# Attention and two token mixtures on one core: preparing the 16 weight blocks of the first mixture on GpSimd in place of ScalarE

## The chip, the cores and the metric

One core of one Trainium2 chip runs the whole program. The metric is the device time of one execution in microseconds (us). The engines are called PE (TensorE, matrix products), PEld (its weight loads), DVE (VectorE), ACT (ScalarE), POOL (GpSimd) and SP (SyncE, which issues most transfers).

## The reference

```python
# 4 batches, 8 heads, 576 tokens, 64 per head; width 512
scores = q @ k.T / 8 + min(-(cum_i - cum_j), 0)      # causal, cum = cumsum(max(s, 0))
x = softmax(scores) @ v                              # heads joined: (4, 576, 512)
h = max(x @ w_in, 0)                                 # first mixture: w_in 512x1024, float64
x = (h * sigmoid(conv3(h))) @ w_out                  # w_out 1024x512, float64
u = x + (x.T @ U @ V).T                              # second mixture: rank 32 along tokens
out = u + max(u @ w_ch1, 0) @ w_ch2                  # 512x2048 and 2048x512, float64
```

The weights of both mixtures arrive as 64-bit floats, so each is read as two 32-bit words and turned into a float32 on the chip. For the products a float32 is split in a high part (rounded to the type fp32r) and a low part (what is left), and three products of the parts are summed.

## The kernel before, in words

The kernel first describes its whole work as a list of operations, each with an engine, an estimated cost and the buffers it reads and writes. A planner then runs a list schedule over it: an engine that becomes free takes, among the operations whose inputs are there by the planner's own clock, the one that stands earliest in the list. The order that comes out is written into each engine's queue and stays fixed: on the chip an engine executes its queue in that order and waits at the head if an input is late. So a changed cost or engine of a few operations can move all others.

The 32 heads of the attention are worked in turn by `att_head(h)`: scores on PE (`products`, line 675, and `last_rows`, line 691), minimum over a row on DVE (`top`, line 636), exponentials on ACT (`exps`, line 653), sums and reciprocals on DVE (lines 726, 727, 768 and 774), multiplication of a row by its reciprocal on POOL (`normalise`, line 664, the tiles P0 to P3 of a head and one tile p for each pair of heads), transposes on PE (line 798), copies of these on ACT (`hi_act`, line 352, tile th), and the products with v (line 824). The x of a pair of heads is split in xh on ACT and xl on POOL (`lo_pool`, line 364). From head 8 on the q and k of a pair are split too: high part on POOL (line 355), low part on DVE (line 361). Eight heads fill one batch; then `m1_in` (line 868) and `m1_out` (line 910) do the first mixture of that batch among the heads of the next.

The weights w_in and w_out of the first mixture come as 16 blocks of 128 x 512 (f = 0 to 7, the columns 0 and 512 of each). `load_split` brings one after the heads that the list W1_AT names (heads 0 to 8 for the first ones, the last four after heads 10 and 11). For each block it does this, in a chain:

1. a transfer of 512 KB into `raw`, of which there are two;
2. `decode64`: the high word of each element, every second 32-bit word of `raw`, is multiplied in place by 2 to the -111 on ACT (line 501); then three integer operations on DVE (line 504 once, line 514 twice) put the float32 together in `wf`, of which there are two as well;
3. `hi_act` (line 352) casts `wf` to the high part on ACT;
4. `lo_pool` (line 364) subtracts the high part from `wf` on POOL.

The high and low parts are w1h and w1l for w_in, and both are called w1o for w_out. `decode64` also serves the weights of the rank-32 step, the convolution and the second mixture, and `load_split` the w_ch2 blocks of the second mixture.

Of the kernel before, what the change touches and what calls it, by code (L numbers as in the profile page):

```python
# [8 lines left out]
F32 = mybir.dt.float32  # L9
# [5 lines left out]
ALU = mybir.AluOpType  # L15
# [293 lines left out]
def tile_attention_moe_mixer(  # L309
# [14 lines left out]
    nc = tc.nc  # L324
# [3 lines left out]
    def dve(n, fn, r, w, fast=False):  # L328
        return plan.op("DVE", (155 if st.get("late") else 70) + n * (0.52 if fast else 1.042), fn, r, w)

    def act(n, fn, r, w, extra=0):
        return plan.op("ACT", (157 if st.get("late") else 53) + n * 0.834 + extra, fn, r, w)

    def pool(n, fn, r, w, two=False, extra=125):
        return plan.op("POOL", ((280 if st.get("late") else 148) + n * 2.1) if two else (37 + n * 0.834 + extra), fn, r, w)

    def dma(nbytes, fn, r, w):
        return plan.op("SP", 640, fn, r, w, late=nbytes / 360)
# [12 lines left out]
    def hi_act(out, src, r, w, n):  # L351
        act(n, lambda: nc.scalar.copy(out(), src()), r, w)  # L352
# [10 lines left out]
    def lo_pool(out, src, hi, r, w, n):  # L363
        pool(n, lambda: nc.gpsimd.tensor_tensor(out(), src(), f32(hi()), ALU.subtract), r, w, two=True)  # L364
# [15 lines left out]
    def ring(pool_, cls, count, shape, dtype, name, at={}):  # L380
        n = at[pool_, cls] = at.get((pool_, cls), -1) + 1
        return pool_.buf(f"{cls}{n % count}", shape, dtype, name)
# [42 lines left out]
    w1h, w1l = {}, {}  # L425
# [59 lines left out]
        o.preds.add(scan)  # L485


    def decode64(out, okeys, raw, n):

        def half(i, dt):
            return raw().bitcast(dt).rearrange("p (n two) -> p n two", two=2)[:, :n, i]

        def oi():
            return out().bitcast(I32)

        act(n, lambda: nc.scalar.mul(half(1, F32), half(1, F32), 2.0**-111), [raw], [(raw, 1)], 40)  # L501
        dve(
            n,
            lambda: nc.vector.tensor_scalar(  # L504
                oi(), half(1, I32), 3, 0x7FFFFFF8, ALU.logical_shift_left, ALU.bitwise_and
            ),
            [(raw, 1)],
            okeys,
            True,
        )  # L510
        for i, sc, op in ((0, 29, ALU.logical_shift_right), (1, -0x80000000, ALU.bitwise_and)):
            dve(
                n,
                lambda i=i, sc=sc, op=op: nc.vector.scalar_tensor_tensor(  # L514
                    oi(), half(i, I32), sc, oi(), op, ALU.bitwise_or
                ),
                [(raw, 1), *okeys],
                okeys,
            )

    def load_split(src, h, l, c, n, name):

        raw = ring(dec, "raw", RINGS["w64"], [128, 512], I64, f"raw_{name}")
        load = dma(n * 1024, lambda: nc.sync.dma_start(out=raw[:, :n], in_=src[:, c : c + n]), [], [raw])
        load.preds.add(st["first"])
        wf = ring(dec, "wf", RINGS["wf"], [128, 512], F32, f"wf_{name}")
        decode64(lambda: wf[:, :n], [wf], raw, n)
        hi_act(lambda: h[:, :n], lambda: wf[:, :n], [wf], [h], n)
        lo_pool(lambda: l[:, :n], lambda: wf[:, :n], lambda: h[:, :n], [wf, h], [l], n)

    def load_cw():
        raw = ring(dec, "raw", RINGS["w64"], [128, 512], I64, "raw_cw")
        dma(24576, lambda: nc.sync.dma_start(out=raw[:, :24], in_=cwU[:, :24]), [], [raw])
        decode64(cw, [cw], raw, 24)
        pool(24, lambda: nc.gpsimd.tensor_scalar(cw(), cw(), 2.0**-8, 1.0, ALU.mult, ALU.mult), [cw], [cw])

    def load_mixu():
        raw = ring(dec, "raw", RINGS["w64"], [128, 512], I64, "raw_mix")
        wf = ring(dec, "wf", RINGS["wf"], [128, 512], F32, "wf_mix")
        dma(163840, lambda: nc.sync.dma_start(out=raw[:, :160], in_=cwU[:, 24:184]), [], [raw])  # L540
        decode64(lambda: wf[:, :160], [wf], raw, 160)
        act(160, lambda: nc.scalar.mul(wf[:, :160], wf[:, :160], 2.0**-8), [wf], [wf])

        def u():
            return wf[:, :160].rearrange("p (a b) -> p a b", b=32)

        hi_dve(lambda: uhl[:, :, 0:32], u, [wf], [(uhl, 0)], 160)
        lo_dve(lambda: uhl[:, :, 32:64], u, lambda: uhl[:, :, 0:32], [wf, (uhl, 0)], [(uhl, 1)], 160)

    def load_mixv(c):  # L550

        raw = ring(dec, "raw", RINGS["w64"], [128, 512], I64, f"raw_v{c}")
        wf = ring(dec, "wf", RINGS["wf"], [128, 512], F32, f"wf_v{c}")
        sl = slice(c, c + HS)
        dma(294912, lambda: nc.sync.dma_start(out=raw[:, :HS], in_=mixV[:, sl]), [], [raw])
        decode64(lambda: wf[:, :HS], [wf], raw, HS)
        act(HS, lambda: nc.scalar.mul(wf[:, :HS], wf[:, :HS], 2.0**-8), [wf], [wf])
        hi_act(lambda: vs[:, sl], lambda: wf[:, :HS], [wf], [(vs, c)], HS)
        low = slice(64, 128)
        lo_dve(  # L560
            lambda: vs[low, sl], lambda: wf[low, :HS], lambda: vs[low, sl], [wf, (vs, c)], [(vs, c)], HS
        )
# [747 lines left out]
    def att_head(h):  # L1310

        if h + 1 < NH:
            if h % 2 == 1:
                prep_v(h + 1)
            if h + 1 in FS:
                prep4(h + 1)
            else:
                if h % 2 == 1:
                    prep(h + 1)
                place(h + 1)  # L1320
        if h == 1:
            decay_parts()
            for t in qkBs:
                clear(t)
        for i in range(2):
            if h < NH:
                scores(h, i)
        if h > 0:
            transp(h - 1, 0)
        if h < NH:  # L1330
            scores(h, 2)
        if h > 0:
            transp(h - 1, 1)
            if h % 2 == 0:
                av(h - 2, 0)
        if h < NH:
            scores(h, 3)
        if h > 0:
            transp(h - 1, 2)
            transp(h - 1, 3)  # L1340
        if h < NH and h % 2 == 0:
            scores4(h)
        if h > 0 and h % 2 == 0:
            av(h - 2, 1)
# [11 lines left out]
    def m1_parts(b):  # L1356

        out = []
        prev = []
        if b:  # L1360
            prev = [(WP, lambda dt=dt: m1_out(b - 1, 1, dt)) for dt in range(KT)]
            last = [(WM, t) for t in mix_parts(b - 1)]
        for f in range(NF1):
            out.append((WI, lambda f=f: m1_in(b, 0, f)))
            if b:
                out += prev[2 * f : 2 * f + 2] if f < 2 else last[2 * f - 4 : 2 * f - 2]
        for f in range(NF1):
            out.append((WI, lambda f=f: m1_in(b, 1, f)))
            if f >= 4:
                out.append((WO, lambda f=f: m1_out(b, 0, f - 4)))  # L1370
        return out

    for h in range(NH + 1):
        b, hh = divmod(h - 1, H)
        todo = []
        if b >= 1:
            parts = m1_parts(b - 1)
            whole = sum(w for w, t in parts)
            at, todo = 0, []
            for w, t in parts:  # L1380
                if hh <= at * H / whole < hh + 1:
                    todo.append(t)
                at += w
        att_head(h)
        for n, (f, c) in enumerate(w1_jobs):
            if h == W1_AT[n]:
                load_split(w1[f], w1h[f, c], w1l[f, c], c, 512, f"w1_{f}_{c}")
        if h == CW_AT:
            load_cw()
        if h == MIX_AT:  # L1390
            load_mixu()
            for c in (0, HS):
                load_mixv(c)
        for t in todo:
            t()
# [82 lines left out]
    for g in range(2):  # L1478
        blk = (w2a, u1p)[g].buf(f"u{g}", [128, 2 * 7 * S], F32R, f"w2_{g}")
        for i in range(7):  # L1480
            f = 7 * g + i
# [3 lines left out]
    def load_w2b(f):  # L1485
        load_split(w2[f], w2h[f], w2l[f], 512, 512, f"w2b_{f}")
# [84 lines left out]
```

## Time and profile before

| | |
|---|---|
| median of 3 runs | 833.66 us (832.91 to 836.38) |
| the profiled execution | 831.95 us, of which 830.2 us is the span from the first to the last instruction |
| granted TensorE clock, mean | 0.996 of full speed |
| PE busy | 791.6 us |
| DVE, ACT, POOL busy | 538.2, 454.3, 360.0 us |

The profile is one execution, recorded instruction by instruction. A busy time counts only executing instructions; the idle time before an instruction is put down to what released it. The ends of matrix products are modelled, so that a PE that counts as busy can still be waiting a little.

### The profile page before, as it was taken

To read this page: it belongs to the slowest core of one execution; us is meant where nothing else is said; L and a number is where in the kernel's file an instruction comes from. 1 tells how busy PE (TensorE), PEld (TensorE's weight loads), DVE (VectorE), ACT (ScalarE), POOL (GpSimd) and SP (SyncE) were. 2 spreads that over 40 slices of the span, in tenths; PEclk is the share of its full clock that TensorE was granted. 3 is DMA by queue.
4 is the path that set the end of the run, shared out by engine and by line. 5 is a ranking of instruction groups with operands and counts; after the bars stand their busy time and mean duration, and the time that the engine had idled before them with its cause. 6 is when DMAs were issued, how large, how long until landed. Compare 5 with 4: busy or idle time off the path is not lost. (4 is left out here: it accounts for less than half of the span.)

```text
span 830.2 us, 15394 instructions
## 1 busy us (share of the span) xinstructions
PE 791.6 (95%) x5300; PEld 709.2 (85%) x5300; DVE 538.2 (65%) x1182; ACT 454.3 (55%) x1144; POOL 360.0 (43%) x441
## 2 busy tenths in 40 slices
PE   4898899999999999999989999999999999999998
PEld 2566788999899999999988898999998888888888
DVE  6887797636855378556998989777688632323232
ACT  4897898858878488767656334324344322222212
POOL 4786684634537234383284776455564200000000
PEclk9999999999999999999999999999999999999999
DMA  7657755734466247030235335446378563636443
GB/s 212 184 170 192 167 154 149 167 97 107 142 144 156 60 111 208 5 109 1 85 109 181 126 133 191 162 150 191 123 220 301 154 193 100 189 103 184 114 127 98
DMA packets 66310, 119.70 MB, mean 144 GB/s; under 512 B 9396, under 2 KB 34868, under 8 KB 66232
## 3 DMA queue, kind: packets, MB, share of 16 engines
q1 hardware_dynamic: 66160, 118.70, 49.7%
q8 instruction: 42, 0.69, 0.4%
q14 instruction: 36, 0.29, 0.1%
q10 hardware_dynamic: 72, 0.01, 0.0%
HBM read 68.81 MB, written 28.90 MB: 118 GB/s over the span
## 5 line engine op out<-in xcount | busy, mean ns | idle before, releaser
L1252 PE MATMUL my<-mh,w 128*128 128x512 f32 (+1 forms) x560 | 158.8, 368 | 0.0
L1153 PE MATMUL ma_S<-u,W 128*128 128x288 f32 x768 | 120.5, 298 | 5.0 <-DVE s L1169 5.0
L1233 DVE SCALAR_TENSOR_TENSOR ml<-ml,mh 128x512 fp32r<-128x512 f32 (+1 forms) x80 | 53.1, 672 | 105.2 <-ACT mh L1230 105.0
L1230 ACT ACTIVATE mh<-ml 128x512 fp32r<-128x512 f32 (+1 forms) x80 | 46.9, 589 | 128.3 <-DMA ml<-ch_d 76.9
L1252 PEld LDWEIGHTS my<-mh,w 128*128 128x128 f32 x560 | 101.7, 189 | 17.5
L910 PE MATMUL y<-gh,w1o 128*128 128x288 f32 x512 | 114.2, 301 | 1.1 <-POOL w1o L364 1.0
L1153 PEld LDWEIGHTS ma_S<-u,W 128*128 128x128 f32 x768 | 108.3, 189 | 7.2 <-DVE s L1169 7.1
L664 POOL TENSOR_SCALAR P<-P,sm 128x128 f32<-128x128 f32 (+3 forms) x128 | 77.1, 618 | 80.3 <-DVE sm L727 63.2
L1252 PE MATMUL my<-ml,w 128*128 128x512 f32 (+1 forms) x280 | 103.0, 368 | 0.0
L1153 PE MATMUL ma_A<-u,W 128*128 128x288 f32 x576 | 92.5, 295 | 0.9 <-ACT p L1165 0.9
L636 DVE CUSTOM_DVE_ANT_0 sc<-sc,mask 128x128 f32<-128x128 f32 (+2 forms) x144 | 68.6, 498 | 34.5 <-PE sc L675 32.5
L910 PEld LDWEIGHTS y<-gh,w1o 128*128 128x128 f32 x512 | 85.0, 188 | 2.2 <-POOL w1o L364 1.3
L364 POOL TENSOR_TENSOR gl<-c,gh 128x288 fp32r<-128x288 f32 x64 | 53.5, 841 | 74.7 <-ACT gh L895 64.4
L868 PE MATMUL h<-xh,w1h 128*128 128x290 f32 x256 | 80.9, 316 | 3.0 <-ACT P L653 0.9
L1153 PEld LDWEIGHTS ma_A<-u,W 128*128 128x128 f32 x576 | 82.0, 188 | 1.6 <-ACT p L1165 1.1
L880 DVE SCALAR_TENSOR_TENSOR c<-h,cw,c 128x288 f32<-128x288 f32 x128 | 64.4, 512 | 26.9 <-ACT c L876 25.8
L868 PE MATMUL h<-xl,w1h 128*128 128x290 f32 x256 | 76.9, 300 | 0.2 <-POOL xl L364 0.2
L868 PE MATMUL h<-xh,w1l 128*128 128x290 f32 x256 | 76.5, 299 | 0.0
L910 PE MATMUL y<-gl,w1o 128*128 128x288 f32 x256 | 74.8, 292 | 0.0
L653 ACT ACTIVATE P<-sc,sm 128x128 f32<-128x128 f32 (+3 forms) x128 | 67.7, 532 | 10.6 <-DVE sm L636 9.2
L352 ACT COPY th<-pt 128x384 f32<-128x384 f32 (+2 forms) x128 | 63.1, 493 | 8.7 <-PE pt L798 7.7
L798 PE MATMUL pt<-ident,P 128*128 128x128 f32 x320 | 59.9, 275 | 1.4 <-ACT th L352 0.8
(139 smaller groups left out, 1734.4 us busy)
## 6 DMA issues: line engine op xcount, KB each, us to landing
ml<-ch_d SPq DMA_DIRECT2D x64, 256.0 KB, 2.8
ch_d<-p SPq DMA_DIRECT2D x64, 144.0 KB, 1.8
raw_w<-w_in SPq DMA_DIRECT2D x16, 512.0 KB, 4.5
raw_w2a<-w_in SPq DMA_DIRECT2D x16, 512.0 KB, 4.8
raw_w2b<-w_in SPq DMA_DIRECT2D x16, 512.0 KB, 4.3
t<-qk_in SPq DMA_DIRECT2D x24, 288.0 KB, 3.1
qkB<-t SPq DMA_DIRECT2D x24, 288.0 KB, 3.8
qkA<-t SPq DMA_DIRECT2D x24, 288.0 KB, 3.9
```

What stands on the lines that cost most here:

```text
L352: act(n, lambda: nc.scalar.copy(out(), src()), r, w)
L364: pool(n, lambda: nc.gpsimd.tensor_tensor(out(), src(), f32(hi()), ALU.subtract), r, w, two=True)
L636: lambda: nc.vector.tensor_tensor_reduce(out=ps[:rows, :w], in0=ps[:rows, :w], in1=mask[:rows, m0 : m0 + w], scale=-0.125, scalar=3.0e38 i ...
L653: lambda: nc.scalar.activation(out(), ps[:rows, :w], ACTF.Exp, bias=low(), scale=-1.0, accum_out=total()),
L664: lambda: nc.gpsimd.tensor_scalar(t[:, :w], t[:, :w], r(), 1.0, ALU.mult, ALU.mult),
L798: nc.tensor.transpose(pt[:, o + rows - 128 : o + rows], d["P"][i][:, 128 * j : 128 * j + 128], turn)
L868: nc.tensor.matmul(ps[:, :W], lhsT=ww, rhs=xx, start=kt + n == 0, stop=kt == KT - 1 and n == 2)
L880: lambda k=k: nc.vector.scalar_tensor_tensor(c(), hh[:, k : k + HS], cw[:, 3 * f + k : 3 * f + k + 1], c(), ALU.mult, ALU.add),
L910: nc.tensor.matmul(ps[:, :HS], lhsT=ww, rhs=xx(), start=f + n == 0, stop=f == NF1 - 1 and n == 2)
L1153: nc.tensor.matmul(ps[:, :HS], lhsT=ww, rhs=uu, start=k == 0, stop=k == 5)
L1233: lambda: nc.vector.scalar_tensor_tensor(ml[:, :n], raw(), 0.0, f32(mh[:, :n]), ALU.max, ALU.subtract),
L1252: nc.tensor.matmul(ys[c][dt][:, :n], lhsT=ww, rhs=xx[:, :n], start=f + k == 0, stop=f == NF2 - 1 and k == 2)
```

## The change

For the 16 blocks of the first mixture alone, the multiplication by 2 to the -111 and the cast to the high part are done by POOL, as `tensor_scalar` instructions with two constants. The three DVE operations, the subtraction on POOL, the transfers and every other use of the two functions stay. The planner is given the costs of `pool(n, ...)` for both, 589 ns for 512 columns, in place of 520 and 480 ns on ACT. Its order of the whole program is made anew from these.

```diff
-    def decode64(out, okeys, raw, n):
+    def decode64(out, okeys, raw, n, spare=False):
...
-        act(n, lambda: nc.scalar.mul(half(1, F32), half(1, F32), 2.0**-111), [raw], [(raw, 1)], 40)
+        if spare:
+            pool(
+                n,
+                lambda: nc.gpsimd.tensor_scalar(half(1, F32), half(1, F32), 2.0**-111, 1.0, ALU.mult, ALU.mult),
+                [raw],
+                [(raw, 1)],
+            )
+        else:
+            act(n, lambda: nc.scalar.mul(half(1, F32), half(1, F32), 2.0**-111), [raw], [(raw, 1)], 40)
...
-    def load_split(src, h, l, c, n, name):
+    def load_split(src, h, l, c, n, name, spare=False):
...
-        decode64(lambda: wf[:, :n], [wf], raw, n)
-        hi_act(lambda: h[:, :n], lambda: wf[:, :n], [wf], [h], n)
+        decode64(lambda: wf[:, :n], [wf], raw, n, spare)
+        (hi_pool if spare else hi_act)(lambda: h[:, :n], lambda: wf[:, :n], [wf], [h], n)
...
-                load_split(w1[f], w1h[f, c], w1l[f, c], c, 512, f"w1_{f}_{c}")
+                load_split(w1[f], w1h[f, c], w1l[f, c], c, 512, f"w1_{f}_{c}", True)
```

## Rows read from the trace of the kernel before

**Rows 1.** The page's busy time, share of the span and instructions of each engine.
```profile
PE 791.6 (95%) x5300; PEld 709.2 (85%) x5300; DVE 538.2 (65%) x1182; ACT 454.3 (55%) x1144; POOL 360.0 (43%) x441
```

**Rows 2.** Busy time by stretch: from:to, length, each engine (instructions), clock, DMA share.
```profile
40.00:60.00 20.00, 18.83 (x125) 12.10 (x125) 16.66 (x48) 18.24 (x51) 16.07 (x21) 1.00 0.57 167
...
83.00:87.00 4.00, 3.68 (x17) 3.67 (x18) 1.39 (x4) 3.11 (x10) 3.12 (x5) 0.57 1.04 207
...
20.00:125.00 105.00, 92.65 (x628) 71.08 (x629) 86.62 (x231) 90.04 (x250) 75.41 (x90) 0.98 0.66 172
...
100.00:125.00 25.00, 22.69 (x167) 20.05 (x164) 22.82 (x56) 23.25 (x63) 20.76 (x22) 1.00 0.56 148
125.00:420.00 295.00, 293.94 (x2230) 271.52 (x2229) 187.77 (x507) 216.84 (x594) 137.32 (x203) 1.00 0.43 113
```

**Rows 3.** Waits of PE, 20 to 125 us: total, times, longest.
```profile
PE pt L798 <- ACT P L653: 2.8, 4, 1.8
...
PE y L910 <- POOL w1o L364: 1.0, 1, 1.0
...
PE h L868 <- ACT x L837: 0.3, 1, 0.3
```

**Rows 4.** ACT by line and shape, 8 to 125 us: busy, mean ns.
```profile
L501 ACT ACTIVATE raw_w<-raw_w 128x512 f32<-128x512 f32 x16 | 11.9, 754 | 0.3 <-DMA raw_w<-w_in 0.2
...
L352 ACT CAST w1o<-wf_w 128x512 fp32r<-128x512 f32 x8 | 5.0, 620 | 1.9 <-DVE wf_w L514 1.9
L352 ACT CAST w1h<-wf_w 128x512 fp32r<-128x512 f32 x8 | 5.0, 619 | 1.2 <-DVE wf_w L514 1.2
```

**Rows 5.** Instructions of single lines or tiles: duration in ns, shortest/median/longest.
```profile
L664 POOL TENSOR_SCALAR p<-p,sm x6: 739/788/1703, 18.2 to 103.3; 128x576 f32<-128x576 f32 x6
...
L355 POOL TENSOR_SCALAR t<-t x8: 670/676/1167, 19.1 to 124.0; 128x576 fp32r<-128x576 f32 x8
...
L364 POOL TENSOR_TENSOR w1l<-wf_w,w1h x8: 1264/1276/1462, 20.2 to 57.0; 128x512 fp32r<-128x512 f32 x8
...
L504 DVE TENSOR_SCALAR wf_w<-raw_w x16: 398/440/1433, 14.9 to 117.7; 128x512 int32<-128x512 int32 x16
```

**Rows 6.** POOL in order of time: start us, us, instructions, idle before.
```profile
27.82 3.07 POOL L664 TENSOR_SCALAR P<-P,sm 128x128 f32<-128x128 f32 x4 [0.44 <-DVE sm L727]
...
35.62 1.20 POOL L364 TENSOR_TENSOR xl<-x,xh 128x576 fp32r<-128x576 f32 x1 [2.12 <-ACT xh L352]
...
40.08 2.05 POOL L664 TENSOR_SCALAR P<-P,sm 128x128 f32<-128x128 f32 x4 [1.86 <-DVE sm L727]
...
77.76 1.28 POOL L364 TENSOR_TENSOR w1o<-wf_w,w1o 128x512 fp32r<-128x512 f32 x1
```

**Rows 7.** DVE in order of time, two places.
```profile
35.68 1.43 DVE L504 TENSOR_SCALAR wf_w<-raw_w 128x512 int32<-128x512 int32 x1
...
77.83 1.84 DVE L361 TENSOR_TENSOR t<-t,t 128x576 fp32r<-128x576 f32 x1
```

**Rows 8.** PE in order of time: the seven places used, with the idle time before.
```profile
24.59 0.52 PE L798 MATMUL pt<-ident,P 128*128 128x128 f32 x3 [0.78 <-ACT th L352]
...
31.37 2.27 PE L824 MATMUL av<-th,vr 128*64 128x320 f32 x20 [0.59 <-ACT th L352]
...
38.70 0.40 PE L868 MATMUL h<-xh,w1h 128*128 128x290 f32 x1 [0.95 <-ACT P L653]
...
53.90 1.12 PE L675 MATMUL sc<-qkF 128*128 128x512 f32 x2 [0.97 <-ACT th L352]
...
81.27 0.30 PE L798 MATMUL pt<-ident,p 128*128 128x128 f32 x1 [1.83 <-ACT P L653]
...
99.64 2.27 PE L824 MATMUL av<-th,vr 128*64 128x320 f32 x20 [1.10 <-ACT th L352]
...
107.58 0.40 PE L868 MATMUL h<-xh,w1h 128*128 128x290 f32 x1 [0.92 <-ACT th L352]
```

**Rows 9.** ACT in order of time: the casts ahead of three of these places.
```profile
23.16 0.62 ACT L352 CAST w1h<-wf_w 128x512 fp32r<-128x512 f32 x1 [0.67 <-DVE wf_w L514]
...
30.37 0.62 ACT L352 CAST w1h<-wf_w 128x512 fp32r<-128x512 f32 x1 [0.53 <-DVE wf_w L514]
...
105.87 0.61 ACT L352 CAST w1o<-wf_w 128x512 fp32r<-128x512 f32 x1
```

## The prediction

> **What bounds the kernel now.** I read the page's busy times first: PE is busy for 95% of the span, no other engine above 65% [rows 1]. So the end can only move by what PE idles, or by the clock that it gets. Next I cut the span into stretches. After 125 us PE is busy for 293.94 of 295 us [rows 2]; nothing of the change happens there, and little is to be had. All 16 blocks are prepared before about 123 us, and in 20 to 125 us PE is busy for 92.65 of 105 us: 12.35 us of idle time. What the change can win on PE lies inside these 12.35 us, plus a stretch of 4 us at 0.57 of the clock (83 to 87 us, behind a PE that had idled just before), which costs 4 x 0.43 = 1.7 us. As later work on PE is back to back, a microsecond won or lost here arrives at the end.
>
> In the same 105 us ACT is busy for 90.04 (86%), DVE for 86.62 (82%) and POOL for 75.41 (72%). ACT is the most loaded of the three, which is the ground for the change. Then I read PE's waits: the eight kinds that name ACT sum to 10.1 us, from 2.8 us down to 0.3 us each, and POOL's w1o has 1.0 us [rows 3]. These names are the last link only. So I followed single idle places back through ACT, DVE and POOL in order of time; they fall in two sorts, used below.
>
> **What the change removes.** From ACT: 16 multiplications of mean 754 ns (11.9 us) and 16 casts of mean 620 ns (10.0 us) [rows 4]. About 20 us of it lies in the stretch of 105 us, so ACT falls from 86% to 67%. That by itself moves nothing; what counts is where PE waited because ACT stood at such an instruction. ACT waited 0.67 us for DVE before the cast at 23.16 us, 0.53 us before the one at 30.37 us, and did another at 105.87 us; the next copies or exponentials queued behind them, and the PE idle times at 24.59, 31.37 and 107.58 us follow [rows 8, 9]. I give the change all three: 0.78 + 0.59 + 0.92 = **2.3 us won**.
>
> **What it adds.** To POOL: 32 instructions on 128 x 512 elements. The trace has no such cast or strided multiplication there, so I bound it. The one-input instruction on 576 columns takes at least 670 ns with constants and 739 ns with a pointer [rows 5]. Four instructions with a pointer, 1280 columns together, take 2.05 us when nothing disturbs them [rows 6]; with 739 ns for 576 columns that is 0.88 ns a column and 0.23 us for each instruction. Then 64 columns fewer than 670 ns are 0.62 us, which I take for the cast. The multiplication touches every second word; nothing on POOL in this stretch does. Below, it costs 0.62 us like the cast; above, 1.26 us, like the subtraction that reads twice as many words [rows 5]. ACT's strided multiplication is dearer than its cast by 0.13 us in the mean [rows 4], and a stride adds no words to be processed, so I take 0.66 us. A block is 1.28 us, and the 15 blocks' worth in the stretch some 18.5 us. POOL rises from 75.4 to 93.9 us of 105 (89%) and takes ACT's place as the most loaded engine but PE.
>
> The Trainium skill, GPSIMD Engine Reference (Engine selection), says that one-input elementwise work on GpSimd runs at roughly line rate, and in its cycle accounting gives 769 ns for a tight loop over 512 elements; with that figure 32 instructions would be an estimated 24.6 us in place of 20.5. The shortest rows here are below it.
>
> Three costs on PE follow.
>
> First, **the shared lock**. DVE's instruction of line 504 takes 398 ns undisturbed, but 1.43 us at 35.68 us, where POOL's xl ran from 35.62 to 36.82 us; line 361 took 1.84 us at 77.83 us, beginning just behind POOL's w1o at 77.76 us [rows 5 to 7]. The reverse shows too: the same four normalising instructions took 2.05 us at 40.08 us and 3.07 us at 27.82 us, where DVE put weights together [rows 6]. Such places precede the PE idle times at 38.70, 53.90, 81.27 and 99.64 us, 4.85 us together [rows 8], through a late minimum on DVE and a late exponential or copy on ACT. They arise from 75.4 us of POOL work; 18.5 us more, in proportion, cost **1.2 us**. A lower bound is nothing (if the new work falls where DVE reads PSUM); an upper one is four times as much, if the new work, which sits right beside DVE's operations on the same block, meets them far more often.
>
> The Trainium skill, SBUF — State Buffer (Who interferes with whom), states the rule: GpSimd and a DVE instruction with two SBUF inputs or in a two-port mode take a shared port pair exclusively, and the later one blocks fully. The trace agrees with it (398 ns against 1.43 us), and it speaks against moving work to GpSimd while DVE decodes.
>
> Second, **POOL's queue at the end of the weights**. In 100 to 125 us POOL is busy for 20.76 of 25 us, which leaves 4.24; four blocks are prepared there and add 4 x 1.28 = 5.1 us. The surplus, **0.9 us**, makes the last w1o later, for which PE already waits 1.0 us [rows 2, 3]. With the locks it would be 1.9 us; at nothing, if PE has heads to work on meanwhile.
>
> Third, **normalisation behind bulk work**. The 11 sets of four normalising instructions and 5 of the p tiles in the stretch will now at times find a new instruction running: its share of time is 18.5/105 = 0.18, what is left of it on average 0.32 us, so 16 x 0.18 x 0.32 = **0.9 us**. The transposes on PE stand behind them. Nothing, where the transposes come later than that anyway.
>
> The three integer operations, the subtraction and the transfers cost what they did. A later decode makes the next transfer into `raw` later by as much, but the next block is not due for a head; if that cover went, SP's later transfers of q and k would wait too. One hop fewer between engines (cast and subtraction both on POOL) I cost at nothing: no one waits for a w1h part before 38.70 us.
>
> **Sum.** -2.3 + 1.2 + 0.9 + 0.9 = +0.7 us. The profiled execution, 831.95 us with a span of 830.2, becomes 832.65. The median of the runs is 1.71 us above the profiled one, so I predict **834.4 us**. A change of this kernel that is under 0.5% (4.2 us) can hardly be told from none, given runs from 832.91 to 836.38 us.
>
> **Rivals.**
>
> *ACT's relief wins (faster).* Exponentials and copies free PSUM banks for PE, and all of them move ahead when ACT falls to 67%. If two thirds of the 10.1 us that name ACT go, and the half-clock stretch with its 1.7 us, less 0.9 us for w1o, the gain is 6.7 + 1.7 - 0.9 = 7.5 us: 826 us. For it speaks that ACT is named most. Against it, that four of the seven places begin with DVE and POOL meeting. It decides if POOL keeps its queue: normalisation must begin as soon after the reciprocal as now (0.44 us and 1.86 us idle before it [rows 6]).
>
> *POOL becomes the bound (slower).* In 40 to 60 us POOL has 16.07 us of work [rows 2] and the four blocks there bring 5.1: 21.2 in 20 us. With the same in 100 to 125 us, the queue is over full in two stretches: 1.2 + 1.9 us; the locks at their upper bound cost 4.8 us, and normalisation behind two new instructions in place of half of one, 16 x 0.18 x 1.28 = 3.7 us. Less 2.3 us, that is +9.3 us: 843 us. It decides once POOL passes some 95% in 20 to 125 us, because then its delay no longer dies out between pairs of heads.
>
> *The strided multiplication costs as much as a subtraction (slower).* 16 x 0.6 us = 9.6 us more, POOL at 93.9 + 14 x 0.6 = 102 of 105 us before any lock. With no slack left PE bears up to all of it: 844 us. Against it, a stride adds no words.
>
> *The order shifts but the waits only change their names.* That is within my forecast: an ACT below its bound does nothing for a PE that is busy for 88% of the stretch and fed by DVE.
>
> **How the numbers follow.** Chances: my forecast (within 0.5%) 0.48, its own range 830 to 838 us; relief 0.23; POOL as the bound 0.22; dear stride 0.07. So faster 0.23, same 0.48, slower 0.29. The range goes from the relief at 826, of which I leave out the far half, to POOL as the bound at 843: 827 to 843 us, with some 0.1 left out on each side.
>
> **What would show it.** In the profile after: no raw_w and w1 instruction on ACT, ACT near 70 us in 20 to 125 us; 32 new one-input instructions on POOL of 0.62 to 0.70 us when alone; POOL above 90% there; lines 504, 514 and 361 on DVE longer in the mean than now; idle times of PE behind casts gone, and new ones that name POOL. PE's idle time to 125 us should be 13 us in place of 12.35. Wrong would be a strided instruction far from 0.66 us; a second stretch at about half the clock, or none; or a POOL that PE waits for more than three times.

## The result and the profile after

The changed kernel takes 844.25 us in the median of four runs (840.59 to 845.87), beside 835.02 us in four runs of the kernel before (832.91 to 837.54). The ratio on record is 1.0124 with the interval [1.0093, 1.0155]; the quotient of the two medians alone is 1.011, and all ratios below are those on record. The change is slower by about 1.2%, some 10 us, and lies 1.25 us above my range. The profiled execution took 840.59 us with a span of 838.8 us, 8.6 us more than before.

The page's busy times after, to be read beside [rows 1]:

```profile
PE 795.7 (95%) x5300; PEld 709.5 (85%) x5300; DVE 541.5 (65%) x1182; ACT 439.7 (52%) x1112; POOL 382.7 (46%) x473
```

ACT lost 14.6 us and POOL got 22.7 us. In the median the single instructions cost what I had worked out (0.66 us for the multiplication, 0.62 us for the cast); in the mean, with what disturbs them, it is 0.71 and 0.64 us. From line 501 on, the lines of the changed kernel are numbered 8 higher: the first operation of DVE's decode, line 504 before, is line 512, and line 504 is now POOL's multiplication (each run below has a numbering of its own). These rows of single instructions give the duration in ns, shortest/median/longest, and the first and last start:

```profile
L504 POOL TENSOR_SCALAR raw_w<-raw_w x16: 637/664/1093, 14.1 to 122.7; 128x512 f32<-128x512 f32 x16
...
L355 POOL TENSOR_SCALAR w1h<-wf_w x8: 610/616/620, 19.0 to 63.2; 128x512 fp32r<-128x512 f32 x8
...
L918 PE MATMUL y<-gh,w1o x512: 288/295/403, 125.7 to 439.3; 128*128 128x288 f32 x171
```

And in the kernel before:

```profile
L910 PE MATMUL y<-gh,w1o x512: 288/296/401, 116.3 to 429.4; 128*128 128x288 f32 x171
```

The y rows date the loss: the first y product begins at 125.7 us, and in the kernel before it began at 116.3 us; in both, 605 PE instructions stand ahead of it. That is 9.4 us, already more than the 8.6 us of the whole span. So everything is lost before some 126 us, where the weights are prepared. The busy times by stretch, with the columns of [rows 2]:

```profile
20.00:24.00 4.00, 3.58 (x15) 2.92 (x14) 3.05 (x9) 1.43 (x4) 3.18 (x6) 0.50 0.53 165
...
40.00:44.00 4.00, 4.00 (x15) 2.39 (x14) 2.91 (x9) 2.22 (x9) 3.59 (x6) 0.62 0.94 256
...
20.00:125.00 105.00, 89.35 (x576) 65.52 (x574) 81.75 (x212) 68.53 (x200) 88.42 (x109) 0.96 0.60 162
125.00:420.00 295.00, 292.12 (x2209) 268.18 (x2209) 188.39 (x513) 216.75 (x595) 140.37 (x208) 1.00 0.43 112
```

In 20 to 125 us PE's idle time grew from 12.35 to 15.65 us, and its mean clock fell from 0.98 to 0.96. Two stretches stand at the lower level of the clock or near it (the first two rows), where the kernel before has one (83 to 87 us [rows 2]). ACT fell to 65% of the stretch. POOL rose to 84%, less than I had forecast, because the same work now takes longer than the stretch. No engine but PE is above 85%, and still PE is fed less well than before. Up to the first y product PE idles 4.4 us more than before and is busy for 5.0 us more with the same 605 instructions. Of these 5.0 us the lower clock is 3.4 (5.1 us lost against 1.7), and the rest lies within time that counts as busy, whose ends are modelled. The clock's part is that of two single executions: over the runs the mean granted clock is 0.993 after and 0.992 in 23 runs of the kernel before, so, as far as is on record, the clock doesn't account for the 1.2%.

PE's waits in 20 to 125 us after (total, times, longest), beside [rows 3]:

```profile
PE sc L699 <- DMA qkF<-cc: 2.5, 1, 2.5
PE sc L683 <- ACT P L661: 2.4, 1, 2.4
PE pt L806 <- ACT P L661: 2.2, 3, 1.3
PE sc L683 <- DMA qkA<-t: 1.9, 2, 1.0
...
PE pt L806 <- POOL p L672: 0.7, 1, 0.7
```

Two kinds stand out. The waits for transfers are new (4.8 us with one of 0.4 us; none in this stretch before), and by name they are more than the 3.3 us of idle time that PE gained; those that name ACT were 10.1 us and are 9.4. And PE hardly names POOL. The engine that does is DVE:

```profile
DVE wf_w L512 <- POOL raw_w L504: 6.4, 5, 1.8
```

This is DVE's wait for the multiplication, at the head of its queue. Its size is not new: before, DVE stood 9.2 us ahead of the same operation, 6.0 of them until POOL's subtraction had read `wf` (the row of line 504 before, shown with e5). It has another cause now and stands elsewhere. The place at 38.08 us shows what it does; here are POOL, DVE, ACT and PE after in order of time (start us, us, then the instructions):

```profile
29.29 2.96 POOL L672 TENSOR_SCALAR P<-P,sm 128x128 f32<-128x128 f32 x4 [1.10 <-DVE sm L735]
...
32.23 0.99 POOL L504 TENSOR_SCALAR raw_w<-raw_w 128x512 f32<-128x512 f32 x1
...
33.25 0.84 DVE L512 TENSOR_SCALAR wf_w<-raw_w 128x512 int32<-128x512 int32 x1 [1.27 <-POOL raw_w L504]
...
34.59 1.76 POOL L364 TENSOR_TENSOR w1l<-wf_w,w1h 128x512 fp32r<-128x512 f32 x1
...
35.22 1.74 DVE L361 TENSOR_TENSOR t<-t,t 128x576 fp32r<-128x576 f32 x1
...
36.89 0.42 DVE L644 CUSTOM_DVE_ANT_0 sc<-sc,mask 128x256 f32<-128x256 f32 x1
...
37.46 0.47 ACT L661 ACTIVATE P<-sc,sm 128x256 f32<-128x256 f32 x1 [2.78 <-DVE sm L644]
...
38.08 0.49 PE L683 MATMUL sc<-qkF 128*128 128x128 f32 x2 [2.45 <-ACT P L661]
```

The multiplication stood on POOL behind four normalising instructions; DVE stood 1.27 us for it, then lost about a microsecond more where line 361 met the subtraction (1.74 us; the shortest of its kind in this kernel takes 0.74 us). A minimum over scores, which needs neither the weights nor the parts of q and k that line 361 makes, was queued behind both; ACT's exponential waited 2.78 us for it, and PE 2.45 us. PE's clock in the 4 us behind that pause was 0.62.

The transfers come by SP's queue. SP after in order of time, and the PE instruction that waits:

```profile
51.49 0.38 SPq L598 DMA_DIRECT2D vr<-vP_in  x1
56.65 0.33 SPq L532 DMA_DIRECT2D raw_w<-w_in  x1
57.07 0.51 SPq L584 DMA_DIRECT2D qkF<-qk_in  x1
57.63 0.59 SPq L586 DMA_DIRECT2D qkF<-cc  x1
58.27 1.30 SPq L591 DMA_DIRECT2D qkF<-cc  x1
...
64.40 0.67 PE L699 MATMUL sc<-qkF 128*64 128x288 f32 x2 [2.55 <-DMA qkF<-cc]
```

From 51.9 to 56.65 us SP stands at a weight transfer that waits for its buffer, that is for the decode of an earlier block (4.7 us, the longest of its kind; 15.6 us in all, 11.4 before). The q and k of the next pair are queued behind it, and PE waits for them. In the kernel before, the same q and k (the eighth of these transfers in both) went out at 50.30 to 52.55 us, ahead of the ninth weight transfer:

```profile
50.30 0.51 SPq L576 DMA_DIRECT2D qkF<-qk_in  x1
...
52.66 2.45 SPq L524 DMA_DIRECT2D raw_w<-w_in  x2
```

### The profile page after: what moved, and what is told of

Read it like the earlier page. It is cut to its first block, busy times and chain, and to the rows that moved or that the text cites. A ratio compares the mean times of both kernels' runs of the same rounds, so it can differ in the third digit from the quotient of the medians.

```text
span 838.8 us, 15386 instructions
## 1 busy us (share of the span) xinstructions
PE 795.7 (95%) x5300; PEld 709.5 (85%) x5300; DVE 541.5 (65%) x1182; ACT 439.7 (52%) x1112; POOL 382.7 (46%) x473
## 5 line engine op out<-in xcount | busy, mean ns | idle before, releaser
L661 ACT ACTIVATE P<-sc,sm 128x128 f32<-128x128 f32 (+3 forms) x128 | 67.8, 532 | 19.2 <-DVE sm L644 16.8
```

The lines of the kernel that those rows point to most:

```text
L661: lambda: nc.scalar.activation(out(), ps[:rows, :w], ACTF.Exp, bias=low(), scale=-1.0, accum_out=total()),
```

## The experiments

The expectations speak of four theories. **A**: POOL's own load costs the time, because other work waits in its queue (A1) or because it meets DVE's instructions (A2). **B**: the new order costs it, above all weight transfers ahead of q and k on SP. **C**: the multiplication is the first link of a block's chain, and DVE's decode waits for it at the head of its queue. **D**: the planner took POOL for faster than it is. A last rival is that it is ACT's relief that is worth nothing. All experiments were timed in five rounds against the kernel before; "POOL" and "PE" are busy us in 20 to 125 us of each run's profile, the same column as above. e1, e5, e9, e10, e11, e13 and e14 have PE, DVE and SP in the order of the kernel before (in e14 with the added copies), e2 in that of the changed kernel. The other eight have an order of their own, and so differ by it as well. The mean granted clock of the runs is 0.990 to 0.995 (0.992 to 0.994 in the kernel before), but 0.987 in e1 and e14 and 0.988 in e8; there a lower clock is part of the loss.

| run | ratio to before | interval | PE | POOL |
|---|---|---|---|---|
| after | 1.0124 | 1.0093 to 1.0155 | 89.35 | 88.42 |
| e1 work moved, old order | 1.0170 | 1.0145 to 1.0196 | 89.16 | 86.19 |
| e2 work on ACT, new order | 1.0149 | 1.0126 to 1.0172 | 87.01 | 67.23 |
| e3 multiplication alone | 1.0094 | 1.0070 to 1.0119 | 89.26 | 79.66 |
| e4 cast alone | 1.0043 | 1.0024 to 1.0062 | 92.56 | 85.75 |
| e5 two idle casts on POOL | 1.0126 | 1.0104 to 1.0147 | 87.06 | 86.80 |
| e6 decode planned later | 1.0058 | 1.0037 to 1.0080 | 92.36 | 97.23 |
| e7 transfers planned later | 1.0145 | 1.0121 to 1.0168 | 88.27 | 83.86 |
| e8 POOL's measured costs | 1.0153 | 1.0127 to 1.0178 | 91.67 | 80.00 |
| e9 one idle cast on POOL | 1.0085 | 1.0062 to 1.0109 | 91.28 | 81.56 |
| e10 memsets on POOL | 1.0164 | 1.0137 to 1.0191 | 87.38 | 87.26 |
| e11 no multiplication, old order | 0.9989 | 0.9970 to 1.0008 | 95.93 | 76.38 |
| e12 subtractions on DVE | 0.9986 | 0.9960 to 1.0011 | 94.97 | 60.06 |
| e13 tiny memsets on POOL | 1.0125 | 1.0092 to 1.0158 | 87.22 | 82.12 |
| e14 longer decode on DVE | 1.0133 | 1.0100 to 1.0167 | 87.93 | 67.51 |
| e15 no multiplication, new order | 1.0066 | 1.0042 to 1.0091 | 89.86 | 73.31 |
| e16 no multiplication, subtractions on DVE | 0.9938 | 0.9916 to 0.9961 | 97.41 | 61.76 |

### Engine and order taken apart (e1, e2)

e1 issues the 32 instructions to POOL, but tells the planner ACT's costs, so that PE, DVE and SP keep the order of the kernel before, instruction by instruction. e2 is the opposite: the planner is told POOL, and ACT executes; those three queues have the order of the changed kernel.

```diff
e1, against the changed kernel
-            pool(
+            act(
                 n,
                 lambda: nc.gpsimd.tensor_scalar(half(1, F32), half(1, F32), 2.0**-111, 1.0, ALU.mult, ALU.mult),
...
+                40,
...
+            act(n, lambda: nc.gpsimd.tensor_scalar(h[:, :n], wf[:, :n], 1.0, 1.0, ALU.mult, ALU.mult), [wf], [h])
e2
+            pool(n, lambda: nc.scalar.mul(half(1, F32), half(1, F32), 2.0**-111), [raw], [(raw, 1)])
...
+            pool(n, lambda: nc.scalar.copy(h[:, :n], wf[:, :n]), [wf], [h])
```

> The 32 instructions run on POOL as in the change, but the planner is told that they are ACT's, with ACT's costs: PE, DVE and SP keep exactly the order of the kernel before, and only the engine differs. Theory A (POOL itself: its queue and its meetings with DVE hold up PE): as slow as the change, 841 to 847 us, PE idle 15 us or more in 20 to 125 us. Theory B (the new order: transfers of weights stand ahead of those of q and k on SP and wait): near the kernel before, 832 to 837 us, and no wait of PE for a q or k transfer.

> The reverse: the order of the change on PE, DVE and SP, but ACT does the 32 instructions. Theory A: near the kernel before, 832 to 837 us, since POOL has its old work. Theory B: as slow as the change, 840 to 846 us, with PE waiting 4 to 5 us for q and k transfers as there.

Each is as slow as the whole change: 845.32 us (+1.7%) and 844.26 us (+1.5%). In e1, where SP issues what it did before in the same order, DVE stands still for the multiplication twice as long as after:

```profile
DVE wf_w L513 <- POOL raw_w L504: 13.5, 9, 2.7
```

So the loss, by A or by C, doesn't need the new order. In e2 POOL has its old instructions (67.23 us of them in the stretch) and ACT 78.96 us, and yet the new order costs the same; PE's waits name the transfers again:

```profile
PE sc L681 <- ACT th L352: 2.9, 3, 2.0
PE pt L804 <- ACT P L659: 2.6, 5, 1.1
PE pt L804 <- ACT th L352: 2.6, 4, 1.0
PE sc L681 <- DMA qkF<-cc: 2.2, 1, 2.2
```

Neither suits the other's conditions: an order made for POOL's timing was run with ACT's. So e2 shows what an order that doesn't fit costs, not what the order costs in the changed kernel. The two losses don't add (3.2% against 1.24%).

### The halves of the change (e3, e4)

e3 moves only the multiplication, e4 only the cast; each is planned anew.

```diff
e3, against the changed kernel
-        (hi_pool if spare else hi_act)(lambda: h[:, :n], lambda: wf[:, :n], [wf], [h], n)
+        hi_act(lambda: h[:, :n], lambda: wf[:, :n], [wf], [h], n)
e4
-        decode64(lambda: wf[:, :n], [wf], raw, n, spare)
+        decode64(lambda: wf[:, :n], [wf], raw, n)
```

> Only the 16 multiplications on POOL, the casts stay on ACT; planned anew. Theory A: POOL has half of the new work, so about half of the loss, 837 to 841 us. Theory B: the multiplication decides when raw is free, so most of the loss, 839 to 845 us, and DVE's first operation still waits for POOL.

> Only the 16 casts on POOL, the multiplications stay on ACT; planned anew. Theory A: the other half, 837 to 841 us. Theory B: the cast stands behind raw's last reader, so raw is free as early as before: 832 to 837 us.

The multiplication costs 0.94% and the cast 0.43%, for almost the same time on POOL. The multiplication stands at the head of a block's chain, with DVE's queue behind it; behind the cast comes POOL's own subtraction. This would speak for C beside A; but each has an order of its own, and the 0.5% between them may be that.

### POOL's load alone (e5, e9)

ACT keeps its work and the order stays that of before. Ahead of each subtraction POOL does two (e5) or one (e9) further casts into the buffer of the low part, which the subtraction then overwrites.

```diff
e5, against the kernel before (e9: range(1))
...
+            def low():
+                for _ in range(2):
+                    nc.gpsimd.tensor_scalar(l[:, :n], wf[:, :n], 1.0, 1.0, ALU.mult, ALU.mult)
+                nc.gpsimd.tensor_tensor(l[:, :n], wf[:, :n], f32(h[:, :n]), ALU.subtract)
...
```

> The kernel before in its own order, ACT doing its 32 instructions; POOL makes two extra casts of 512 columns into the low part ahead of each subtraction, which overwrites them. So POOL carries the load of the change, but the multiplication, DVE's decode and the cast do not wait for it. Theory A (POOL's load and its meetings with DVE): 841 us or more. Theory C (the multiplication is the first link of the chain: DVE's decode, in its fixed order, waits for POOL, and minima stand behind it): 832 to 838 us, and no wait of DVE for a multiplication.

> The kernel before in its own order, with one extra cast on POOL ahead of each of the 16 subtractions in place of two: half the load. Theory A, if POOL's load costs in proportion: half of 1.26%, 836 to 839 us. If POOL has slack up to some load: 831 to 834 us, and the loss comes with the second cast alone.

Work that nobody asked for, on an engine that was 72% busy, costs 1.26%, as much as the change; half of it costs 0.85%. One place of e5 in order of time shows how:

```profile
83.91 2.22 POOL L533 TENSOR_SCALAR w1o<-wf_w 128x512 fp32r<-128x512 f32 x2 [2.04 <-DVE wf_w L514]
...
85.57 0.15 DVE L783 RECIPROCAL sm<-sm 128x1 f32<-128x1 f32 x1
...
86.21 1.31 POOL L534 TENSOR_TENSOR w1o<-wf_w,w1o 128x512 fp32r<-128x512 f32 x1
...
87.51 1.17 POOL L673 TENSOR_SCALAR p<-p,sm 128x576 f32<-128x576 f32 x1
...
88.74 0.33 PE L807 MATMUL pt<-ident,p 128*128 128x128 f32 x1 [2.42 <-POOL p L673]
```

The reciprocal for p is there at 85.72 us. POOL is at two extra casts and the subtraction until 87.5 us, so the normalisation is 1.8 us late, and PE stands 2.42 us for it. This is A1, but only a part of the 2.42 us is new: in the kernel before the same PE instruction waits 1.83 us, for an exponential (81.27 us [rows 8]). A2 is there as well in e5: DVE's operations on the blocks get longer. In these groups from 8 to 140 us, of before, of e9 and of e5, the numbers behind the bar are busy us and the mean in ns:

```profile
L514 DVE SCALAR_TENSOR_TENSOR wf_w<-raw_w,wf_w 128x512 int32<-128x512 int32 x32 | 26.9, 842 | 0.5
L504 DVE TENSOR_SCALAR wf_w<-raw_w 128x512 int32<-128x512 int32 x16 | 10.1, 630 | 9.2 <-POOL w1l L364 4.0 <-POOL w1o L364 2.0 <-ACT raw_w L501 1.9
```

```profile
L514 DVE SCALAR_TENSOR_TENSOR wf_w<-raw_w,wf_w 128x512 int32<-128x512 int32 x32 | 28.7, 899 | 0.5
L504 DVE TENSOR_SCALAR wf_w<-raw_w 128x512 int32<-128x512 int32 x16 | 10.6, 664 | 10.0 <-issue 4.2 <-ACT raw_w L501 3.6 <-POOL w1l L533 2.1
```

```profile
L514 DVE SCALAR_TENSOR_TENSOR wf_w<-raw_w,wf_w 128x512 int32<-128x512 int32 x32 | 33.5, 1048 | 0.5
L504 DVE TENSOR_SCALAR wf_w<-raw_w 128x512 int32<-128x512 int32 x16 | 8.4, 528 | 9.9 <-POOL w1l L533 4.4 <-POOL w1o L533 2.3 <-ACT raw_w L501 2.0
```

The sum of the two is 37.0 us before, 39.3 in e9 and 41.9 in e5. In e9 line 361, which meets POOL too, got shorter (from 8.8 to 7.7 us), and the 128x4 sums stayed (314 ns each after 319), so these groups together took about 1 us more there, against 7.1 us of time (0.85%). That would speak for the queue. But PE idles only 13.72 us of the stretch in e9, 1.4 us more than before (17.94 us in e5), at a clock of 0.96 against 0.98, so its profile shows little of the queue's cost. One profile of each is what this rests on.

### Queue or meetings (e10, e13, e14)

e10 and e13 were meant to load POOL without DVE meeting it: memsets, which read nothing, in place of e5's casts (three of 512, 512 and 256 columns, or forty of two columns, overwritten again). e14 is the reverse: POOL keeps its old work, and DVE does a 320-column copy of the first integer operation once more ahead of each block.

```diff
e10, in the function of e5 (e13: forty memsets of 2 columns)
+                for m in (n, n, n // 2):
+                    nc.gpsimd.memset(f32(l[:, :m]), 0.0)
e14, against the kernel before
+            if wone:
+                nc.vector.tensor_scalar(
+                    oi()[:, :320], half(1, I32)[:, :320], 3, 0x7FFFFFF8, ALU.logical_shift_left, ALU.bitwise_and
+                )
```

> As with two extra casts, but POOL writes constants instead (512, 512 and 256 columns, some 1.3 us for each block), so it reads nothing while it is busy. Theory A1 (the queue: normalisation and subtractions stand behind the new work): 841 to 845 us, as with the casts. Theory A2 (meetings with DVE's reads): 831 to 835 us, and DVE's second and third operations on a block back at the durations of the kernel before.

> As with two extra casts ahead of each subtraction, in the order of the kernel before, but POOL makes 40 memsets of two columns instead, some 1.2 us for a block by the 0.03 us from start to start that such memsets take at the head of the kernel, so that no single one can hold DVE for long. Theory A1 (the queue): 840 to 845 us with DVE's three operations on a block at 37 us in sum, as in the kernel before. Theory A2 (meetings with DVE): 831 to 835 us.

> The kernel before in its own order, with DVE's first operation on each of the 16 blocks preceded by one on 320 columns that it overwrites: some 0.3 us for a block, 4.9 us in all, which is what the two extra casts made DVE's operations on the blocks longer. POOL's load is the old one. Theory A2 (DVE's lengthening is what PE pays for): 839 to 843 us. Theory A1: 832 to 836 us.

The memsets cost 1.64% and 1.25%. But DVE's meetings didn't stay as they were; the first operation got longer, in e10:

```profile
L504 DVE TENSOR_SCALAR wf_w<-raw_w 128x512 int32<-128x512 int32 x16 | 13.0, 811 | 10.0 <-POOL w1l L533 4.4 <-POOL w1o L533 2.4 <-ACT raw_w L501 2.0
```

With line 514 (29.4 us) the sum is 42.4 us, and 42.7 us in e13, more than in e5. Most of it isn't the memsets' doing: in e10 four of the 16 met a subtraction of these blocks and took 1.02 to 1.45 us, while of the five that met memsets alone four took 0.42 to 0.49 us, and one 0.85 us. So neither tells A1 from A2. e14 adds more to DVE than planned (7.7 us for the 16 copies, with their gaps and meetings some 9.5 us in the four groups), leaves POOL at 67.51 us, and costs 1.33%. So a delay on DVE without new work on POOL, twice as long as e5's (9.5 us against 4.9), is enough for the whole loss, in part by the lower clock of its runs; and by e9 a load on POOL with about 1 us on DVE is enough for two thirds of it. In the changed kernel itself DVE's two groups grew by only 2.4 us (28.4 + 11.0 against 37.0), so meetings are probably not its larger part; the shares stay open. A load on POOL that DVE never meets was not found.

### The plan's part (e6, e7, e8)

All three are the changed kernel with another plan. In e6 the planner believes that the multiplication's result comes 1.5 us later, so it puts other work on DVE ahead of the decode. In e7 a block's transfer is planned no earlier than the subtraction two blocks before it, so that SP has less to wait for. In e8 the planner is given POOL's costs as measured.

```diff
e6, against the changed kernel
-            )
+            ).late = 1500
e7
...
+        if spare and len(subs) > 1:
+            load.preds.add(subs[-2])
...
e8
...
+            plan.ops[-1].cost += 190
...
+                extra=254,
...
+            extra=388 if st.get("slow") else 208,
```

> The change, with the planner told that the multiplication's result arrives 1.5 us later on every other engine, so that DVE's decode is put later in its queue. Theory C: DVE's 6.4 us of waiting for the multiplication go to under 2 us and the time to 834 to 840 us. Theory A: no better than the change, 841 to 847 us, since POOL does as much.

> The change, with the transfer of a block put on SP no earlier than the planner's end of the subtraction of the block two before. Theory B (weight transfers wait on SP ahead of those of q and k): SP's 15.6 us of waiting for the decode shrink by half, PE waits for no q or k transfer, and the time is 836 to 841 us. Theories A and C: 841 to 847 us, as POOL and the decode are where they were.

> The change, with the planner given POOL's costs as the changed kernel's trace has them while weights are prepared: 718 and 644 ns for multiplication and cast, 180 ns more for each normalising instruction, 190 ns more for a subtraction. Theory D (the order is bad because the planner's POOL is too fast): 833 to 839 us. Theory A: 841 to 847 us.

e6 gives back half of the loss (0.58% remains): DVE's wait for the multiplication falls from 6.4 to 2.0 us, POOL reaches 97.23 of 105 us, and PE 92.36 us, almost what it had before. That agrees with C for about half; but e6 has a new order throughout, and what that is worth by itself isn't shown. e7 cuts SP's wait for the decode from 15.6 to 5.6 us, but POOL then waits 6.5 us for the blocks, and the time stays at +1.45%. PE still waits 5.2 us for q and k there, so e7 didn't remove what B speaks of:

```profile
PE sc L689 <- DMA qkB<-t: 3.1, 1, 3.1
...
PE sc L705 <- DMA qkF<-cc: 2.1, 1, 2.1
```

That B isn't needed for a loss is shown by e1, where PE waits for no transfer in the stretch; how much it is in the changed kernel stays open. e8 doesn't help either (+1.53%): POOL waits 6.5 us for blocks there too, PE 7.7 us for q and k, and PE's clock in the stretch is 0.90. A plan by POOL's measured costs is no better: D falls.

### What ACT's relief is worth (e11, e15), and the other way about (e12, e16)

e11 takes the 16 multiplications off every engine: one more exponent bit is cleared by line 504's mask, and the factors of two later ACT instructions become 1.0 and 0.5, so that these blocks are not scaled by an instruction of their own (this serves a narrower range of weights). The order stays that of before. e15 does the same, but is planned without the multiplications. e12 moves the 16 subtractions from POOL to DVE, and e16 is e15 and e12 together.

```diff
e11, e15 and e16, against the kernel before
-                oi(), half(1, I32), 3, 0x7FFFFFF8, ALU.logical_shift_left, ALU.bitwise_and
+                oi(), half(1, I32), 3, 0x3FFFFFF8 if wone else 0x7FFFFFF8, ALU.logical_shift_left, ALU.bitwise_and
e12 and e16
-        lo_pool(lambda: l[:, :n], lambda: wf[:, :n], lambda: h[:, :n], [wf, h], [l], n)
+        (lo_dve if name.startswith("w1") else lo_pool)(
```

> The kernel before in its own order without the 16 multiplications on any engine: DVE's mask takes the exponent bits that they removed, and the two later factors that undo their scaling are set to fit, so ACT loses 11.9 us of work and POOL gets none. If ACT was the bound of these 105 us: 825 to 829 us. If ACT's load is nothing to PE, as the first step of the change supposed wrongly: 831 to 834 us.

> The kernel before without the 16 multiplications on any engine (DVE's mask takes the exponent bits, the later factors are set to fit), now planned without them. If ACT's load matters once the planner knows of it: 825 to 829 us. If not: 829 to 834 us.

> The opposite of the change: the kernel before with the 16 subtractions of these blocks on DVE, which takes 21.6 us from POOL and gives DVE some 11 us; planned anew. Theory A (POOL's load is what PE pays for): 826 to 831 us. If DVE's queue is as tight as POOL's: 834 to 842 us.

> The same without the multiplications, and the 16 subtractions on DVE: ACT loses 11.9 us, POOL 21.6 us, DVE gains some 11 us; planned anew. If POOL's load is what PE pays for and DVE has room: 823 to 828 us, faster than both kernels. If DVE's queue is then the bound: 830 to 836 us.

e11 costs POOL nothing and frees ACT of 11.9 us of the multiplications, and the time is the same as before (-0.11%, interval -0.30 to +0.08, so a gain of 2.5 us is not excluded). PE's idle time in the stretch falls to 9.07 us, but the clock is 0.95 there:

```profile
20.00:125.00 105.00, 95.93 (x644) 74.74 (x642) 89.48 (x234) 83.14 (x240) 76.38 (x91) 0.95 0.62 172
```

That is 3.3 us less idle time and, by the clock, 3.2 us more lost, in this one profile; over its 12 runs the clock is 0.991, and 0.992 in the kernel before. e15 has the same instructions in an order made for them, and is 0.8% slower than e11: what the planner's order is worth varies by as much as the effects looked for. e12 takes load off POOL (60.06 us) and gives DVE 92.67 us; no change can be told. e16 is the only one that beats both kernels: 828.48 us, -0.62% (interval -0.84 to -0.39), with POOL at 61.76 and PE at 97.41 us:

```profile
20.00:125.00 105.00, 97.41 (x657) 74.61 (x656) 95.86 (x264) 84.06 (x245) 61.76 (x77) 0.97 0.63 175
```

e16 and e12 differ by the multiplications, which leave ACT, and by the order; POOL's load is nearly the same. So e16's gain over e12 (0.48%) is ACT's relief or the order, and not POOL's relief. What the runs show is that work came off POOL without loss, DVE at 91% included, and went onto it only with loss.

## Why the prediction was wrong, step by step

**Right**: where the bound is (PE before 125 us, nothing to be had after); the single prices (0.66 and 0.62 us forecast, 0.664 and 0.616 measured); that the strided multiplication isn't dear. ACT's busy time (near 70 us forecast, 68.53 measured) is right in part by luck, as the stretch now holds 576 PE instructions in place of 628. The sum has the right sign (slower) with wrong terms on both sides. One slip changes no term by 0.1 us: 15 blocks of 1.28 us are 19.2 us, not 18.5.

**The terms that failed** are the three costs of POOL's load, 1.2 + 0.9 + 0.9 = 3.0 us. e5 measures as much load in the order of before, placed ahead of the subtractions: 1.26%, 10.5 us. I had scaled the meetings with DVE in proportion, and had let normalisation wait for 0.32 us in 18% of the cases. Ahead of the PE instruction at 88.74 us of e5 it waits 1.8 us, because the extra work comes in bundles with the subtraction, just when a block is ready, and not spread evenly. And I counted each delay once, at its place: a late link holds what is queued behind it on DVE, then on ACT, then on PE, as at 38.08 us, and the clock in the 4 us behind that pause was 0.62. What each part of this costs in the changed kernel isn't shown.

**The relief**, -2.3 us, was given for idle places whose last link was a late ACT copy or exponential behind a cast. e11 takes the multiplications away and gains nothing that can be told. The casts' own relief wasn't measured alone; e4, which relieves ACT of them and loads POOL, is slower by 0.43%. PE's waits that name ACT hardly fell with the change (10.1 to 9.4 us). ACT was the most loaded engine, but by these runs not what set PE's pace.

**What I costed at nothing.** "A later decode makes the next transfer into `raw` later by as much, but the next block is not due for a head": the cover was gone at 56.65 us, and PE's new waits for transfers are 4.8 us. I had named this case and given it no price. I let the new order cost nothing as well ("the order shifts but the waits only change their names"); e2 and e15 against e11 show that an order can be worth 0.8 to 1.5%. And I priced no wait of DVE for the multiplication on a fuller queue (6.4 us after, in place of 9.2 us for other things; 13.5 us in the old order of e1).

**The rivals.** "POOL becomes the bound" gave 843 us, close to 844.25, and its price was about right. Its condition was not: it was to decide once POOL passes some 95% of the stretch, and POOL stands at 84%; in e6, where POOL does reach 93%, the kernel is faster than the changed one. So its number came out near partly by luck. A queue in a fixed order cost time here well before it was full. ACT's relief and the dear stride didn't come.

**The signs.** PE's idle time is 15.65 us, where I had 13. Of the signs of being wrong the clock's came, two stretches near its lower level in place of one; a PE that names POOL more than three times didn't (twice, 1.1 us). Of the other signs POOL above 90% didn't come; DVE's lines 504 and 514 got longer in the mean (692 and 893 ns after 630 and 842), but line 361 shorter (998 after 1094).

What stays open: how the loss divides between POOL's queue and its meetings with DVE, how much of it is the transfers on SP, and how much the order alone, since e1 and e2 each show the full loss and don't add.

## What to carry to other kernels

A low busy share is no room in a queue whose order is fixed: ask for each added instruction which urgent one stands behind it, and price its whole length there, not its share of the time. Where a planner makes the order anew, run the move in the old order first, and the new order with the old engines, before believing either; here the order alone was worth up to 1.5% (e2). And count no relief of the busiest engine before you have taken its work away altogether and seen the end move.

## What the runs showed of the hardware that I had not expected

POOL instructions that read nothing can still hold up DVE, and short ones in a row do so too. In e13 line 504 on DVE, which takes some 0.4 us undisturbed, began beside xl, and it ended only when all forty memsets of two columns (98 ns each) behind xl had ended:

```profile
38.14 1.55 POOL L364 TENSOR_TENSOR xl<-x,xh 128x576 fp32r<-128x576 f32 x1 [1.25 <-ACT xh L352]
...
38.55 2.61 DVE L504 TENSOR_SCALAR wf_w<-raw_w 128x512 int32<-128x512 int32 x1
...
39.64 1.24 POOL L533 MEMSET w1l<- 128x2 f32 x40
```

The two-input line 514, which casts in e5 had lengthened from 842 to 1048 ns in the mean, came to 922 ns with memsets in e10 and 894 ns in e13. The Trainium skill, SBUF — State Buffer (Who interferes with whom), says that a two-input DVE instruction contends with GpSimd's reads but not with one that only writes, while the two-port mode contends with GpSimd altogether; these means agree with it in direction.

The fastest of the kernels was the one with the most work on DVE, 95.86 of 105 us in e16, though DVE is the engine that I had taken to suffer most from the change.
